# A single maximum in the second step of every unit of a two-branch attention kernel

## The chip, the cores and the metric

One Trainium2 chip, one core of it. The metric is the device time of the kernel in microseconds (us). The kernel before takes 1472.81 us, the median of 3 runs from 1471.78 to 1473.0 us.

## The reference

Two attention branches read the same input `x` of 2048 rows by 512 columns and are mixed by a gate per row. Branch A is a dilated window attention (each row sees 8 keys, every second row back). Branch B, which fills most of the time, is full attention of 32 query heads of 16 columns on one shared key head and one shared value head:

```python
def _A_ref(x, wqkv, wo):                       # 32 heads of 16, W, dil = 8, 2
    idx = pos[:, None] - off[None, :]          # off = arange(8) * 2
    logits = jnp.einsum("bhsd,bhswd->bhsw", q, kg) * scale
    o = jnp.einsum("bhsw,bhswd->bhsd", _softmax(logits), vg)
    return o @ wo
def _B_ref(x, wq, wk, wv, wo):                 # 32 query heads, one key and one value head
    scores = jnp.einsum("bhqd,bkd->bhqk", q, k) * (Dh ** -0.5)
    o = jnp.einsum("bhqk,bkd->bhqd", _softmax(scores), v)
    return o @ wo
g = _sigmoid((x * gate_w).sum(-1, keepdims=True))
return g * a + (1 - g) * b
```

The weights of branch B's queries and keys are 8 times the others, so its scores are large, and the kernel subtracts each row's own maximum before the exponential.

## The kernel before, in words

**Stages.** A front part (until about 284 us in the trace) splits the inputs into a high and a low part, projects queries, keys and values, and begins the maxima. A long loop then does branch B step by step, with branch A's arithmetic on GpSimd (POOL) beside it. Three times in the loop a block of output projections (`out_phase`) is put between two steps, and a short tail projects the last rows.

**Units and steps.** Branch B is cut into 32 units: a unit is 512 query rows of 4 heads. A unit has 16 steps, one for each block of 128 keys, so the loop runs over `s` from 0 to 512 with `u, kt = divmod(s, 16)`. The engines' work of one step is recorded in this order:

- two times the scores of a pair of heads, two matmuls into the bank pair `pe` (L465), which ScalarE turns into `pexp` with one exponential of 128x1024 (L471);
- between the first and the second of these the maxima of a later unit: always, where slots are left, a *pair* of maxima, two matmuls into `pm` (L322) and one reduction of 128x1024 on VectorE (`fill_pair`, L344), and sometimes a *single* maximum, one matmul into `ps` (L322) and one reduction of 128x512 (`fill_one`, L356);
- at the end the weighted sums of the step before, eight matmuls into `po` (L480), which accumulate over the 16 steps of a unit. In the trace one `po` row of eight matmuls therefore closes each step, and the time from one such row to the next is the length of a step.

**The turn of a unit.** In step `s % 16 == 0` the sixteenth weighted sum of the old unit is recorded and right behind it `finish_a`: VectorE transposes `po` to `tt` (L494) and takes a reciprocal (L500). The first weighted sum of the new unit, at the end of step `s % 16 == 1`, may overwrite `po` only when that transpose has read it. I call step `s % 16 == 1` the turn step, and count turns by the unit that begins: turn 14 is step 225.

**When a unit's maxima are complete** (64 slots, counted in `left`), `filled` puts a small reduction (`ms`, L332) and a transpose (`mt`, L334) on VectorE; ScalarE and GpSimd make the shift rows of it, and eight small DMAs write them into the unit's query tile.

**What sets the order.** Nothing is scheduled after recording: each engine works its list in the order in which the Python code records it. That order comes from a planner. `clk` holds a guess of each engine's time, `free[bank]` the time at which a bank may be written again, `slots` and `half` the maxima that are still to be done. In the loop `order` is (first scores, "m2", "m1", second scores): "m2" is the pair, "m1" the single. The single is given out when `singles(s)` says yes and the bank `ps` is free by the planner's clock; each one given lowers `owing` by 1. `singles` adds to `owing`, at every step, the maxima left beyond what the pairs of the remaining steps (1.94 each) and the coming output blocks (15.5 a row block) will take, divided by the steps left. It says no in step 0 of a unit, where `owing` is below 1, and where the planner has VectorE over 1.5 us behind TensorE while `owing` is below 2. In the turn step the pair's reduction stands behind the transpose on VectorE, so the planner has VectorE far behind there, and that last rule decides.

A place where DMAs are issued within the loop is `run_tasks` (the shift rows, L453, and query loads, L290 and L291, on SyncE's queue) and `run_pool` (branch A); both run by the planner's clock.

Of the kernel before, what the change touches and what calls it, by code (L numbers as in the profile page):

```python
# [48 lines left out]
def gated_mix_kernel(ctx, tc, xt, wa, wk, wq, wo_a, wo_b, out):  # L49
# [274 lines left out]
    def to_go():  # L324
        return 2 * len(slots) + len(half)
# [519 lines left out]
    def singles(s):  # L845

        steps = 16 * (NU - 1) - 8 - s
        if steps <= 0 or to_go() <= 0:
            return to_go() > 0
        owing[0] += (to_go() - 1.94 * steps - 15.5 * (NJ - 4 - outs)) / steps  # L850
        owing[0] = min(owing[0], 3.0)
        if s % 16 == 0 or owing[0] < 1.0 or clk["dve"] - clk["pe"] > 1.5 and owing[0] < 2.0:
            return False
        return True
# [373 lines left out]
    for s in range(NS + 1):  # L1228
# [29 lines left out]
        for which in order:  # L1258
            if which == "m2":
                if slots or half:  # L1260
                    fill_ready("m2", M2S)
                else:
                    next(tail, None)
            elif which == "m1":
                if singles(s) and fill_ready("m1", M1S):
                    owing[0] -= 1.0
            elif s < NS:
                exp_pair(s, which)
# [84 lines left out]
```

## Time and profile before

| | |
|---|---|
| median of 3 runs | 1472.81 us |
| the profiled execution | 1471.12 us, span 1469.1 us |
| busy: TensorE, VectorE, ScalarE, GpSimd | 1454.6, 1141.9, 1303.6, 951.1 us |
| clock granted to TensorE | 1.0 throughout |
| exponentials of branch B | 1024, 1.02 us each |
| transposes of `po` at a turn | 31, 0.72 us each |

In the timeline a row is a run of like instructions: start and length in us, engine, line, operation, output and inputs, and how many; a bracket at its end gives the idle time before it and what ended that. PE is TensorE, PEld its weight loads, DVE VectorE, ACT ScalarE. Matmuls are pipelined, so a TensorE that is shown as busy all the time may still be waiting inside a step; the length of a step is read from the starts.

### The profile page before, as it was taken

How to read it: one execution, taken by the hardware profiler on the slowest of the kernel's cores; microseconds unless marked ns; L12 is line 12 of the kernel's file. 1: busy time of each engine (PE TensorE's matmuls, PEld its weight loads, DVE VectorE, ACT ScalarE, POOL GpSimd, SP SyncE). 2: the span in 40 equal slices, each digit the busy share in tenths (PEclk: the TensorE clock that was granted, in tenths of full speed). 3: DMA queues.
4: the chain of work that ended last, by engine and by line, in shares of the span. 5: the costliest groups of instructions: out<-in, count | busy, mean ns of one | idle time of the engine just before them, and what ended most of it. 6: DMA issues, size and time to landing. Idle time of an engine off the chain costs nothing.

```text
span 1469.1 us, 29512 instructions
## 1 busy us (share of the span) xinstructions
PE 1454.6 (99%) x10965; PEld 739.7 (50%) x10965; DVE 1141.9 (78%) x1837; ACT 1303.6 (89%) x1706; POOL 951.1 (65%) x1693
## 2 busy tenths in 40 slices
PE   9999999999999999999999999999999999999998
PEld 6899999733333333333333373333333743383334
DVE  6778888788888888788888877888888778778821
ACT  5888988799999999999999989999999889889994
POOL 5731898888988988889888898898851311150000
PEclk9999999999999999999999999999999999999999
DMA  6653342320211210102202111121100000000000
GB/s 225 170 169 113 101 149 68 117 73 25 71 41 49 78 49 31 68 22 69 78 12 71 42 63 46 45 71 41 42 12 12 27 16 2 1 31 1 1 2 29
DMA packets 43912, 85.67 MB, mean 58 GB/s; under 512 B 9520, under 2 KB 25960, under 8 KB 39672
## 3 DMA queue, kind: packets, MB, share of 16 engines
q1 hardware_dynamic: 36632, 44.79, 9.9%
q0 software_dynamic: 6560, 37.95, 7.7%
q8 instruction: 86, 1.41, 0.4%
q10 hardware_dynamic: 576, 1.05, 0.2%
q14 instruction: 58, 0.48, 0.1%
HBM read 57.97 MB, written 25.25 MB: 57 GB/s over the span
## 4 chain that ended last, share of the span: by engine, by line
PE 94%; ACT 2%; POOL 1%; DVE 1%; DMA 1%; issue 1%; SPq 0%; POOLq 0%; ACTq 0%
PE po L480 34%; PE pe L465 25%; PE pf L1082 10%; PE pm L322 8%; PE ps L322 5%; PE pe L780 5%; PE pd L393 3%; PE po L322 1%; ACT pexp L471 1%; PE pf L193 1%; PE pe L1283 1%; DMA ad<-stage 0%; DVE mx L344 0%; DMA xraw<-xt 0%; PE pm L836 0%
## 5 line engine op out<-in xcount | busy, mean ns | idle before, releaser
L471 ACT ACTIVATE pexp<-pe 128x1024 f32<-128x1024 f32 x1024 | 987.8, 1023 | 67.6 <-PE pe L465 63.3
L344 DVE TENSOR_REDUCE mx<-pm 128x2 f32<-128x1024 f32 x475 | 580.1, 1221 | 174.6 <-PE pm L322 172.3
L480 PE MATMUL po<-pexp,vst 128*32 128x512 f32 x4096 | 545.5, 605 | 0.1
L465 PE MATMUL pe<-qst,kst 64*128 64x512 f32 x1984 | 523.3, 459 | 4.6 <-ACT pexp L471 2.5
L465 PEld LDWEIGHTS pe<-qst,kst 64*128 64x128 f32 x1984 | 208.8, 183 | 451.6 <-ACT pexp L471 427.2
L405 ACT ACTIVATE dd<-pd 128x512 f32<-128x512 f32 x367 | 209.0, 604 | 44.7 <-PE pd L393 30.9
L356 DVE TENSOR_REDUCE mx<-ps 128x1 f32<-128x512 f32 x333 | 226.5, 680 | 4.5 <-PE ps L322 1.8
L322 PE MATMUL ps<-kst,qst 62*128 62x512 f32 x503 | 206.5, 410 | 0.1
L322 PE MATMUL pm<-kst,qst 62*128 62x512 f32 x916 | 185.9, 397 | 0.4
L542 POOL TENSOR_TENSOR pr<-aext 128x256 f32<-128x256 f32 x256 | 182.0, 737 | 4.9 <-DMA aext<-ad 4.6
L602 POOL TENSOR_TENSOR oa<-oa,av 128x256 f32<-128x256 f32 x224 | 164.1, 732 | 15.8
L480 PEld LDWEIGHTS po<-pexp,vst 128*32 128x32 f32 x4096 | 80.6, 108 | 170.3 <-issue 161.8
L417 DVE CUSTOM_DVE_ANT_0 dd<-ps,dd 128x512 f32<-128x512 f32 x185 | 127.7, 690 | 34.2 <-PE ps L322 14.2
L417 DVE CUSTOM_DVE_ANT_0 dd<-po,dd 128x512 f32<-128x512 f32 x182 | 125.6, 690 | 29.8 <-PE po L322 12.9
L599 POOL TENSOR_TENSOR av<-aext,lg 128x256 f32<-128x256 f32 x224 | 139.3, 622 | 12.8
L393 PE MATMUL pd<-kd,qst 62*128 62x512 f32 x367 | 143.5, 401 | 2.5 <-ACT dd L405 2.5
L1082 PE MATMUL pf<-wal,xh 64*128 64x384 f32 (+1 forms) x496 | 127.9, 338 | 0.0
L1082 PE MATMUL pf<-wah,xh 64*128 64x384 f32 (+1 forms) x496 | 124.0, 337 | 0.0
L1082 PE MATMUL pf<-wah,xl 64*128 64x384 f32 (+1 forms) x496 | 122.7, 338 | 0.0
L322 PEld LDWEIGHTS ps<-kst,qst 62*128 62x128 f32 x503 | 92.9, 185 | 43.5 <-DVE mx L356 38.6
L506 POOL TENSOR_TENSOR rl<-rl,gate_t 128x16 f32<-128x16 f32 x31 | 6.9, 222 | 157.9 <-DVE rl L500 157.9
L322 PEld LDWEIGHTS pm<-kst,qst 62*128 62x128 f32 x916 | 88.3, 186 | 3.5 <-DVE mx L344 3.0
(199 smaller groups left out, 1725.4 us busy)
## 6 DMA issues: line engine op xcount, KB each, us to landing
aext<-ad POOLq DMA_DIRECT2D x32, 1056.0 KB, 5.4
ad<-stage SPq DMA_DIRECT2D x32, 384.0 KB
qst<-qd SPq DMA_DIRECT2D x62, 128.0 KB
xraw<-xt SPq DMA_DIRECT2D x16, 256.0 KB
qd<-qhi SPq DMA_DIRECT2D x16, 256.0 KB
qd<-qlo SPq DMA_DIRECT2D x16, 256.0 KB
qst<-qd SPq DMA_DIRECT2D x62, 64.0 KB
qst<-ml SPq DMA_DIRECT2D x220, 2.0 KB
```

Of the source, the lines that this page charges most:

```text
L322: nc.tensor.matmul(dst, qst[place(v)][b:b + 62, pr, t * P:(t + 1) * P], kst[b:b + 62, kc * 512:(kc + 1) * 512], start=True, stop=True)
L344: got = nc.vector.tensor_reduce(m[:, :, pr, t, kc], dst, AX.X, ALU.max)
L356: got = nc.vector.tensor_reduce(m[:, odd, pr, t, kc:kc + 1], dst, AX.X, ALU.max)
L393: nc.tensor.matmul(dst, qst[place(v)][b:b + 62, pr, t * P:(t + 1) * P], kd[0][b:b + 62, kc // 2, :], start=True, stop=True)
L405: got = nc.scalar.activation(held[b][k], dst, AF.Relu)
L417: got = nc.vector.tensor_tensor_reduce(held[b][k], dst, held[b][k], 1.0, -FMAX, ALU.add, ALU.max, m[:, b, pr, t, kc:kc + 1])
L465: nc.tensor.matmul(bank[:, odd, :], kst[b:b + 64, kt * P:(kt + 1) * P], qst[place(u)][b:b + 64, pr, :], start=True, stop=True)
L471: got = nc.scalar.activation(e, bank, AF.Exp, scale=SCALE)
L480: nc.tensor.matmul(po[32 * i:32 * i + 32, :], vst[:, kt, :], pexp[s, i // 2][:, i % 2, :], start=(kt == 0), stop=(kt == NJ - 1))
L542: nc.gpsimd.tensor_mul(pr[:, k], q, e[:, o:o + NH, AC:2 * AC])
L602: nc.gpsimd.tensor_add(ao, ao, av)
L1082: inst = nc.tensor.matmul(home(x)[0][:, :n], l[h], r[h], start=(i == 0 and b == 0), stop=(i == 3 * C - 1 and b == 1))
```

## The change

In `singles`, a step with `s % 16 == 1` says yes before the other rules are asked:

```diff
         owing[0] += (to_go() - 1.94 * steps - 15.5 * (NJ - 4 - outs)) / steps
         owing[0] = min(owing[0], 3.0)
+        if s % 16 == 1:
+            return True
         if s % 16 == 0 or owing[0] < 1.0 or clk["dve"] - clk["pe"] > 1.5 and owing[0] < 2.0:
             return False
         return True
```

Counted in the recorded programs, the change does this. There are 30 turn steps in which maxima are left; three of them follow an output block and had a single before and after. Of the other 27, 9 had a single before, and all 27 have one now. Outside the turn steps the loop has fewer singles: 300 before and 273 after in the steps 17 to 486, without the nine steps around the output blocks. In all, singles in `ps` go from 325 to 316, full pairs from 475 to 480, half-filled pair banks from 10 to 7, and the three output blocks take 66, 57 and 60 maxima before and 59, 66 and 60 after. The output blocks stay at steps 272, 400 and 448, and the last maximum at step 488.

TensorE around turn 14, before; the first row is the last weighted sums of the old unit, and `ps` is the single:

```order
L480 MATMUL po<-pexp,vst 32x512 x4
L465 MATMUL pe_4182<-qst_80,kst 128x512 x2
L322 MATMUL pm<-kst,qst_77 128x512 x2
L465 MATMUL pe_4183<-qst_80,kst 128x512 x2
L480 MATMUL po<-pexp,vst 32x512 x4
L465 MATMUL pe_4182<-qst_80,kst 128x512 x2
L322 MATMUL pm<-kst,qst_77 128x512 x2
L322 MATMUL ps<-kst,qst_77 128x512
L465 MATMUL pe_4183<-qst_80,kst 128x512 x2
L480 MATMUL po<-pexp,vst 32x512 x4
```

The same place after:

```order
L480 MATMUL po<-pexp,vst 32x512 x4
L465 MATMUL pe_4182<-qst_80,kst 128x512 x2
L322 MATMUL pm<-kst,qst_77 128x512 x2
L322 MATMUL ps<-kst,qst_77 128x512
L465 MATMUL pe_4183<-qst_80,kst 128x512 x2
L480 MATMUL po<-pexp,vst 32x512 x4
L465 MATMUL pe_4182<-qst_80,kst 128x512 x2
L322 MATMUL pm<-kst,qst_77 128x512 x2
L465 MATMUL pe_4183<-qst_80,kst 128x512 x2
L480 MATMUL po<-pexp,vst 32x512 x4
```

The single stood in the step behind the turn step and stands now in the turn step itself, ahead of the second scores.

VectorE around turn 15, before; `tt<-po` is the transpose for which the new unit's first weighted sum waits, and `ms` and `mt` are what a completed unit of maxima puts on the engine:

```order
L356 TENSOR_REDUCE mx<-ps 128x1
L344 TENSOR_REDUCE mx<-pm 128x2
L494 STREAM_TRANSPOSE tt<-po 128x512
L500 RECIPROCAL rl<-tt 128x16
L344 TENSOR_REDUCE mx<-pm 128x2
L332 TENSOR_REDUCE ms<-mx 128x32
L334 STREAM_TRANSPOSE mt<-ms 128x32
L344 TENSOR_REDUCE mx<-pm 128x2
```

The same place after:

```order
L356 TENSOR_REDUCE mx<-ps 128x1
L344 TENSOR_REDUCE mx<-pm 128x2
L332 TENSOR_REDUCE ms<-mx 128x32
L334 STREAM_TRANSPOSE mt<-ms 128x32
L494 STREAM_TRANSPOSE tt<-po 128x512
L500 RECIPROCAL rl<-tt 128x16
L344 TENSOR_REDUCE mx<-pm 128x2
L356 TENSOR_REDUCE mx<-ps 128x1
```

The unit's maxima are now complete one step earlier, so `ms` and `mt` stand ahead of the transpose. They stand so at turns 3 and 6 before, and at turns 3, 6, 9, 12 and 15 after; at 3, 6 and 12 the reduction ahead of them is a half pair, at 9 and 15 a full one.

Branch A's small reductions on VectorE, the shift rows and the query loads move by some rows with the planner's clock; their number stays.

## The prediction

> **What bounds the kernel now.** I began with the page, then read the loop by windows, the waits, and last the timeline of TensorE and VectorE around several turns. Of the page, two lines, and under them one row of the windows by stage (busy time and count of TensorE, its weight loads, VectorE, ScalarE, GpSimd, then the granted clock):
>
> ```profile
> span 1469.1 us, 29512 instructions
> ...
> L471 ACT ACTIVATE pexp<-pe 128x1024 f32<-128x1024 f32 x1024 | 987.8, 1023 | 67.6 <-PE pe L465 63.3
> ```
>
> ```profile
> 460.00:560.00 100.00, 100.00 (x709) 35.93 (x709) 82.71 (x101) 94.72 (x105) 87.48 (x169) 1.00 0.17 55
> ```
>
> TensorE is shown busy all the time at full clock, ScalarE for 94.7 of 100 us and VectorE for 82.7. So neither of the two others is full, and ScalarE's 67.6 us of idle time ahead of its exponentials is mostly time in which it waits for TensorE's scores. TensorE's busy share doesn't say how much it waits inside a step; the starts do. This is the timeline of TensorE around turn 14, where the turn step has no single:
>
> ```profile
> 748.60 1.06 PE L480 MATMUL po<-pexp,vst 128*32 128x512 f32 x8
> ...
> 749.93 0.39 PE L322 MATMUL pm<-kst,qst 62*128 62x512 f32 x2
> 750.16 0.40 PE L465 MATMUL pe<-qst,kst 64*128 64x512 f32 x2
> 750.49 1.07 PE L480 MATMUL po<-pexp,vst 128*32 128x512 f32 x8
> ...
> 751.83 0.39 PE L322 MATMUL pm<-kst,qst 62*128 62x512 f32 x2
> 752.15 0.49 PE L465 MATMUL pe<-qst,kst 64*128 64x512 f32 x2
> 752.57 1.06 PE L480 MATMUL po<-pexp,vst 128*32 128x512 f32 x8
> ...
> 754.14 0.39 PE L322 MATMUL ps<-kst,qst 62*128 62x512 f32 x1
> ...
> 754.70 1.06 PE L480 MATMUL po<-pexp,vst 128*32 128x512 f32 x8
> ...
> 756.27 0.45 PE L322 MATMUL ps<-kst,qst 62*128 62x512 f32 x1
> ...
> 756.88 1.06 PE L480 MATMUL po<-pexp,vst 128*32 128x512 f32 x8
> ```
>
> From one `po` row to the next is one step. The step of 750.49 has no single and takes 750.49 - 748.60 = 1.89 us. The turn step has the same matmuls and takes 752.57 - 750.49 = 2.08. The two steps behind it each have a single and take 2.13 and 2.18. So the turn step loses 0.19 us without doing anything for it: its second scores begin 0.32 behind the pair instead of 0.23 (they wait for ScalarE to empty their bank), and its weighted sums begin 0.42 behind those scores instead of 0.33 (they wait for the transpose of `po`). Two rows of the waits name both:
>
> ```profile
> PEld pe L465 <- ACT pexp L471: 441.2, 562, 1.7
> ...
> PEld po L480 <- DVE tt L494: 6.8, 25, 0.4
> ```
>
> Now turn 5, which already carries a single in the turn step:
>
> ```profile
> 448.07 1.06 PE L480 MATMUL po<-pexp,vst 128*32 128x512 f32 x8
> ...
> 449.97 1.06 PE L480 MATMUL po<-pexp,vst 128*32 128x512 f32 x8
> ...
> 451.54 0.39 PE L322 MATMUL ps<-kst,qst 62*128 62x512 f32 x1
> ...
> 452.09 1.06 PE L480 MATMUL po<-pexp,vst 128*32 128x512 f32 x8
> ...
> 453.99 1.06 PE L480 MATMUL po<-pexp,vst 128*32 128x512 f32 x8
> ```
>
> Its three steps take 1.90, 2.12 and 1.90 us. The single is in the turn step and costs 0.04 there, and the step behind it, now without one, takes 1.90. That is the change in small, within the trace of before.
>
> **The change part by part.** All sums are against the profiled execution's own 1471.12 us (span 1469.1 and 2.0 around it). The median is 1.7 above that; I subtract the same sum from it.
>
> *Singles that enter a turn step: 18.* These are the first and the last of the 18 turn steps without one, each with a step with a single behind it:
>
> ```profile
> 315.96 1.07 PE L480 MATMUL po<-pexp,vst 128*32 128x512 f32 x8
> ...
> 318.05 1.06 PE L480 MATMUL po<-pexp,vst 128*32 128x512 f32 x8
> ...
> 320.19 1.06 PE L480 MATMUL po<-pexp,vst 128*32 128x512 f32 x8
> ```
>
> ```profile
> 1381.40 1.07 PE L480 MATMUL po<-pexp,vst 128*32 128x512 f32 x8
> ...
> 1383.51 1.07 PE L480 MATMUL po<-pexp,vst 128*32 128x512 f32 x8
> ...
> 1385.63 1.06 PE L480 MATMUL po<-pexp,vst 128*32 128x512 f32 x8
> ...
> 1387.53 1.07 PE L480 MATMUL po<-pexp,vst 128*32 128x512 f32 x8
> ```
>
> They take 2.09 and 2.11, over the 18 a mean of 2.10. The nine turn steps with a single take 2.12 to 2.14, a mean of 2.13. So 18 x 0.03 = +0.5 us.
>
> *Singles that leave other steps: 27.* Outside the turn, the steps with a single take 2.14 where the step before has none (113 of them; above 2.14, 2.13, 2.12) and 2.17 where it has one (185; above 2.18), together 2.16. The 134 steps without take 1.91 (above 1.89, 1.90, 1.90). A single is worth 0.25 there. Of the 27, 25 stood beside a pair: -25 x 0.25 = -6.3. The other two stood alone, where no pair was ready, and become steps with a pair alone: about -0.1 together. 18 of the 27 are the ones that moved to the turn. The other nine are no longer needed as singles, since five more steps have a full pair, three fewer have a half one, and the output blocks take two more maxima.
>
> *The output blocks: two maxima more.* The 916 matmuls of pairs bound that:
>
> ```profile
> L322 PE MATMUL pm<-kst,qst 62*128 62x512 f32 x916 | 185.9, 397 | 0.4
> ```
>
> 185.9 / 916 = 0.20 us each on TensorE; between 0, if they fill gaps of the block, and 0.4. I take +0.2.
>
> *VectorE in the turn step.* Its queue is what the single's reduction joins. VectorE at turn 5, with the single:
>
> ```profile
> 449.85 1.23 DVE L344 TENSOR_REDUCE mx<-pm 128x2 f32<-128x1024 f32 x1 [0.31 <-PE pm L322]
> 451.11 0.72 DVE L494 STREAM_TRANSPOSE tt<-po 128x512 f32<-128x512 f32 x1
> 451.86 0.25 DVE L500 RECIPROCAL rl<-tt 128x16 f32<-128x16 f32 x1
> 452.03 1.16 DVE L344 TENSOR_REDUCE mx<-pm 128x2 f32<-128x1024 f32 x1
> 453.11 0.67 DVE L356 TENSOR_REDUCE mx<-ps 128x1 f32<-128x512 f32 x1
> 453.86 1.23 DVE L344 TENSOR_REDUCE mx<-pm 128x2 f32<-128x1024 f32 x1
> 455.75 1.23 DVE L344 TENSOR_REDUCE mx<-pm 128x2 f32<-128x1024 f32 x1 [0.66 <-PE pm L322]
> ```
>
> The single's reduction stands behind the transpose, so the weighted sums do not wait for it. Behind it on the engine stand the next step's pair and whatever needs `pm` and `ps` again. The work from the transpose to the end of the next step's pair is 0.72 + 0.25 + 1.16 + 0.67 + 1.23 = 4.03 us, against 2.12 + 1.90 = 4.02 of TensorE for these two steps: VectorE comes out even, and two steps later it is idle for 0.66 us again. I take the cost at nothing; the cover is that the step behind has no single, which holds in all 27 turns after. Without that cover it is a wait of up to one reduction, 0.67. The Trainium skill's page "TensorEngine Tiling (Array Packing)", section "PSUM Bottleneck", says that tiling speeds up TensorE but not the emptying of PSUM, which can then become the bottleneck; by that rule the turn would be paid by VectorE, and the sum would lose what the first rival below takes from it. The nine turns with a single speak against it: the steps behind them take a mean of 1.91, like any other step without one.
>
> *The transpose comes later at two turns.* At turns 9 and 15 `ms` and `mt` are now ahead of `tt`, behind a full pair. Turn 6 shows them behind a half pair:
>
> ```profile
> 482.92 0.69 DVE L356 TENSOR_REDUCE mx<-pm 128x1 f32<-128x512 f32 x1
> 483.65 0.29 DVE L332 TENSOR_REDUCE ms<-mx 128x32 f32<-128x128 f32 x1
> 483.97 0.21 DVE L334 STREAM_TRANSPOSE mt<-ms 128x32 f32<-128x32 f32 x1
> 484.19 0.72 DVE L494 STREAM_TRANSPOSE tt<-po 128x512 f32<-128x512 f32 x1
> ```
>
> From the end of the half pair, 483.61, to the transpose they take 0.58. A full pair is 0.54 longer than a half one, and after it the transpose starts at once (451.08 and 451.11 above), so it comes some 0.55 later at these two turns. With the single as cover, 0.1 of that may be hidden: 2 x 0.45 = +0.9, between 0 and 1.1. At turn 12 the pair is a half one, and nothing is lost.
>
> *Other queues.* Query loads and shift rows swap places by a few rows on SyncE's queue, and branch A's pieces move on GpSimd's. They are meant for units that start several steps later, so I take nothing for them, between -0.5 and +1.
>
> *The steps with a single that are left.* They stand behind another single less often, 151 of 273 instead of 185 of 298, so that their mean is (122 x 2.14 + 151 x 2.17) / 273 = 2.157 instead of 2.159: 273 x 0.002 = -0.5.
>
> The sum: 0.5 - 6.3 - 0.1 + 0.2 + 0.9 - 0.5 = -5.3. That is 1465.8 us for a run like the profiled one, and 1472.8 - 5.3 = **1467.5** for the median.
>
> **The rivals.**
>
> *VectorE pays (the same time).* Where branch A's small reductions fall between the turn and the next steps, VectorE does not come out even, and the next pair or single waits for its bank. If each of the 18 new turn singles cost a full 0.25 in that way, 4.5 of the 5.3 us come back: 1472.8 - 0.8 = 1472.0. For it: the 4.03 against 4.02 above. Against it: the steps behind the nine turns, and the 0.66 us of idle time right after. The rule of the skill's page named above points here.
>
> *ScalarE is the limit (slower).* The single stands ahead of the second scores, so the second exponential of the turn step can start 0.23 later. If ScalarE has no slack to catch up, the single costs its full 0.25 there, 18 x 0.25 = +4.5. Steps that lose a single then run into ScalarE's pace: a plain step behind a plain step takes 2.08 at turn 14, not 1.91, so that 27 removed singles bring only 27 x (2.16 - 2.08) = -2.2. With +0.2 and +0.9 that is +3.4, so 1476.2. It decides from where the exponentials follow each other without idle time over a whole unit. For it: ScalarE's 94.7 of 100 us. Against it: the 5.3 us that are left, which are spread over all units, and turn 5, where three steps in a row run at 1.90, 2.12 and 1.90.
>
> That the change does not do what it says can be left out: the order has the single in all 27 turn steps.
>
> **How the numbers follow.** My forecast gets 0.78, VectorE 0.14, ScalarE 0.08. The forecast's own range: without the late transposes and with the other queues at their good end it is -5.3 - 0.9 - 0.5 = -6.7, so 1466.1, and 1.7 lower, 1464.4, if the runs fall as the profiled one did; with the two maxima, the transposes and the queues at their bad ends it is -5.3 + 0.2 + 0.2 + 1 = -3.9, and if a quarter of the 5.3 is lost to what I don't see, -2.6, so 1470.2. I take 1464.4 to 1471.2 as the range, which reaches a little towards VectorE's case. A measurement of this kernel can tell about 0.2% from no change, 2.9 us, so faster begins below 1469.9: 0.78, of which I give 0.02 to the same for the forecast's own upper end, so 0.76; the same 0.16 with VectorE's case; slower 0.08.
>
> **What would show it right or wrong.** In the profile after, the 18 turn steps should take 2.13 and the steps behind them 1.90; turns 9 and 15 some 2.5; 27 fewer steps of 2.16; ScalarE's idle time ahead of its exponentials should fall by some 5 us. I am wrong if the turn steps with a single take 2.3, if the steps behind them take 2.1 with a wait for L344 or L356 in front, or if plain steps elsewhere rise to 2.08.

## The result, and the profile after

| | before | after |
|---|---|---|
| median | 1472.99 us (1470.65 to 1474.68) | 1467.71 us (1465.41 to 1468.85) |
| ratio, 95% interval | | 0.9965 (0.9956 to 0.9974) |
| the profiled execution | 1471.12 us | 1466.79 us, span 1464.7 us |

The kernel is 5.3 us faster, by the medians of eight runs each. The page after, its span and the exponentials' group:

```profile
span 1464.7 us, 29500 instructions
...
L471 ACT ACTIVATE pexp<-pe 128x1024 f32<-128x1024 f32 x1024 | 986.8, 1023 | 64.2 <-PE pe L465 58.4
```

ScalarE's idle time ahead of its exponentials, behind TensorE's scores, went from 63.3 to 58.4 us. This is TensorE around turn 14 after the change, the `po` rows and the single:

```profile
746.36 1.07 PE L480 MATMUL po<-pexp,vst 128*32 128x512 f32 x8
...
748.25 1.06 PE L480 MATMUL po<-pexp,vst 128*32 128x512 f32 x8
...
749.82 0.40 PE L322 MATMUL ps<-kst,qst 62*128 62x512 f32 x1
...
750.38 1.07 PE L480 MATMUL po<-pexp,vst 128*32 128x512 f32 x8
...
752.27 1.06 PE L480 MATMUL po<-pexp,vst 128*32 128x512 f32 x8
...
754.39 1.06 PE L480 MATMUL po<-pexp,vst 128*32 128x512 f32 x8
```

The four steps take 1.89, 2.13 (the turn step, with its single), 1.89 and 2.12 us. Before, the same four took 1.89, 2.08, 2.13 and 2.18. VectorE at the same turn:

```profile
748.13 1.23 DVE L344 TENSOR_REDUCE mx<-pm 128x2 f32<-128x1024 f32 x1 [0.29 <-PE pm L322]
749.38 0.72 DVE L494 STREAM_TRANSPOSE tt<-po 128x512 f32<-128x512 f32 x1
...
751.38 0.67 DVE L356 TENSOR_REDUCE mx<-ps 128x1 f32<-128x512 f32 x1
752.15 1.23 DVE L344 TENSOR_REDUCE mx<-pm 128x2 f32<-128x1024 f32 x1
```

The single's reduction stands behind the transpose, as the order says, and the next pair's reduction starts at 752.15, 0.1 behind its end.

I took every step's length from the starts of the `po` rows over the whole loop: steps 17 to 486 without the nine around the output blocks, 461 steps, as in the prediction. Number x mean, in us:

| steps | before | after |
|---|---|---|
| turn step, plain | 18 x 2.097 | none |
| turn step with a single | 9 x 2.127 | 27 x 2.147 |
| other step with a single, behind a plain step | 113 x 2.143 | 122 x 2.141 |
| other step with a single, behind one with a single | 185 x 2.172 | 151 x 2.182 |
| other step with a single but no pair | 2 x 1.984 | none |
| plain step, behind one with a single | 125 x 1.898 | 151 x 1.903 |
| plain step, behind a plain step | 9 x 2.077 | 10 x 2.055 |
| sum | 960.7 | 956.6 |

The 151 steps hold one of 3.71 us. The same step takes 2.12 in a second profile of the change, so it costs some 1.6; it is the granted clock that falls there, as the last section shows. Without it the loop gains 5.7 us. From profiled execution to profiled execution the 4.4 us of span are: -5.7 in these steps, +1.6 by the long step, +0.5 in the output blocks, -0.2 up to the first `po` row, and the -0.5 that is left in the first 15 steps, beside the blocks, in the last steps and in the tail.

### The profile page after: what moved, and what is told of

It reads as the page before. It is cut to its first block, busy times and chain, and to the rows that moved or that the text cites. A ratio compares the mean times of both kernels' runs of the same rounds, so it can differ in the third digit from the quotient of the medians.

```text
span 1464.7 us, 29500 instructions
## 1 busy us (share of the span) xinstructions
PE 1451.1 (99%) x10965; PEld 742.0 (51%) x10965; DVE 1140.7 (78%) x1832; ACT 1303.8 (89%) x1708; POOL 950.9 (65%) x1693
## 4 chain that ended last, share of the span: by engine, by line
PE 95%; ACT 1%; POOL 1%; DVE 1%; DMA 1%; issue 0%; SPq 0%; POOLq 0%; ACTq 0%
PE po L480 34%; PE pe L465 25%; PE pf L1084 10%; PE pm L322 8%; PE ps L322 6%; PE pe L780 5%; PE pd L393 3%; PE po L322 1%; PE pf L193 1%; PE pe L1285 1%; ACT pexp L471 1%; DVE mx L344 0%; DMA ad<-stage 0%; DMA xraw<-xt 0%; PE pm L836 0%
## 5 line engine op out<-in xcount | busy, mean ns | idle before, releaser
L471 ACT ACTIVATE pexp<-pe 128x1024 f32<-128x1024 f32 x1024 | 986.8, 1023 | 64.2 <-PE pe L465 58.4
L344 DVE TENSOR_REDUCE mx<-pm 128x2 f32<-128x1024 f32 x480 | 586.5, 1222 | 173.8 <-PE pm L322 169.7
L465 PE MATMUL pe<-qst,kst 64*128 64x512 f32 x1984 | 515.7, 459 | 4.4 <-ACT pexp L471 2.6
L465 PEld LDWEIGHTS pe<-qst,kst 64*128 64x128 f32 x1984 | 204.1, 184 | 454.6 <-ACT pexp L471 424.8
L356 DVE TENSOR_REDUCE mx<-ps 128x1 f32<-128x512 f32 x323 | 219.7, 680 | 2.8 <-PE ps L322 2.8
L322 PE MATMUL ps<-kst,qst 62*128 62x512 f32 x494 | 202.0, 409 | 0.1
```

What stands on the lines that cost most here:

```text
L322: nc.tensor.matmul(dst, qst[place(v)][b:b + 62, pr, t * P:(t + 1) * P], kst[b:b + 62, kc * 512:(kc + 1) * 512], start=True, stop=True)
L344: got = nc.vector.tensor_reduce(m[:, :, pr, t, kc], dst, AX.X, ALU.max)
L356: got = nc.vector.tensor_reduce(m[:, odd, pr, t, kc:kc + 1], dst, AX.X, ALU.max)
L465: nc.tensor.matmul(bank[:, odd, :], kst[b:b + 64, kt * P:(kt + 1) * P], qst[place(u)][b:b + 64, pr, :], start=True, stop=True)
L471: got = nc.scalar.activation(e, bank, AF.Exp, scale=SCALE)
```

## The experiments

Each was run beside the kernel before, on one chip per group; a ratio is to the kernel before in the same group. "Singles" are the single maxima, and the edits are in the planner's rule that gives them out.

**The place or the number? Two kernels.** The change also makes the singles more regular and fewer. The first kernel forbids them in the turn step:

```diff
         if s % 16 == 1:
-            return True
+            return False
```

> No unit's turn step has a single at all (27 of 27 without, before 18 of 27); the planner gives 328 singles elsewhere (before 325) and four maxima fewer in the output blocks. My theory (a single costs 0.03 us in a turn step and 0.25 elsewhere): 9 turn steps lose 0.03 each, some 12 more ordinary steps carry a single at 0.25, four maxima fewer in the blocks at 0.12: +2.2 us, so 1475.2 against 1473.0 before. Rival, the gain came from the planner's other changes and not from the place: 1472.5 to 1473.5.

Measured: 1475.67 us (1474.12 to 1478.24), ratio 1.0026 (1.0017 to 1.0036), 3.5 slower than before. The turn steps are plain in all 27 turns. At turn 10 step 0 of the unit takes unusually long; TensorE there, `po` rows alone:

```profile
615.00 1.07 PE L480 MATMUL po<-pexp,vst 128*32 128x512 f32 x8
...
617.28 1.06 PE L480 MATMUL po<-pexp,vst 128*32 128x512 f32 x8
...
619.18 1.07 PE L480 MATMUL po<-pexp,vst 128*32 128x512 f32 x8
```

617.28 - 615.00 = 2.28 for step 0, and 1.90 for the plain turn step behind it. Four of the 27 turns are like this (10, 16, 20 and 23, with 2.06 to 2.28 and then 1.90 to 1.92). So a turn step without a single need not take 2.08; that was the first sign against a part of my reading.

The second kernel forces a single in the middle of the unit instead:

```diff
-        if s % 16 == 1:
+        if s % 16 == 8:
```

> The same forced single, but in the ninth step of each unit, far from the turn; the turn steps follow the old rules (7 of 27 with a single). My theory: no place is gained, 1473.0 to 1474.0. Rival, a regular single in any fixed step evens out the planner's bookkeeping and that is the gain: 1467 to 1468.5.

Measured: 1473.62 us (1472.72 to 1475.42), ratio 1.0012 (1.0003 to 1.0021). The turn steps stay at 20 x 2.078 and 7 x 2.110 us and the steps' sum is 962.4. As regular as the change, and slower than before: regularity alone brings nothing. The number of singles is not held apart here (311 in the 461 steps, 309 before, 300 in the change); the kernel with the late transposes below does that.

**VectorE left out of it.** The change as it is, but the single of the turn step gets no reduction (31 reductions fewer; TensorE's list stays the same):

```diff
+        if bare:
+            after("dve", after("pe", 0, T_R) + T_LAT, T_RED1)
+            free[key] = clk["dve"] + 0.08
+            filled(v, 1)
+            return
...
+                bare[:] = [1] * (s % 16 == 1)
```

> As the changed kernel, but the reduction of the single given in a turn step is left out (31 reductions of 128x512 on VectorE, so those maxima are missing from the result); TensorE's list is the same. My theory (VectorE takes the turn's single at almost no cost): 0 to 0.8 us faster than the changed kernel, 1466.9 to 1467.7. Rival, VectorE pays for the turn's singles: a further 2 to 4.5 us faster, 1463.2 to 1465.7.

Measured: 1466.68 us (1465.74 to 1468.18), ratio 0.9964 (0.9952 to 0.9977); the change itself has 0.9965. TensorE at turn 14 (the weighted sums are L487 in this file):

```profile
749.80 1.06 PE L487 MATMUL po<-pexp,vst 128*32 128x512 f32 x8
...
751.37 0.40 PE L322 MATMUL ps<-kst,qst 62*128 62x512 f32 x1
...
751.93 1.07 PE L487 MATMUL po<-pexp,vst 128*32 128x512 f32 x8
...
753.83 1.07 PE L487 MATMUL po<-pexp,vst 128*32 128x512 f32 x8
```

2.13 and 1.90 us, within 0.01 of what the full change takes there, and 27 turn steps at a mean of 2.148, with 1.932 for the steps behind them (2.147 and 1.933 in the change). The reduction is hidden, and the rival in which VectorE pays for the turn's single is out. The Trainium skill's rule that emptying PSUM can become the bottleneck ("TensorEngine Tiling (Array Packing)", section "PSUM Bottleneck") does not bind in the change.

**A single in step 0 as well.** If singles are cheap at a turn, two may be cheaper, unless the reduction ahead of the transpose delays it:

```diff
-        if s % 16 == 1:
+        if s % 16 < 2:
```

> A single is given in the first step of a unit as well as in the second. Its reduction of 0.68 us then stands ahead of the transpose of the finished sums. My theory: the singles that leave other steps save about 7.5 us against before, but the turn's weighted sums wait some 0.5 to 0.65 longer in 27 turns (+13 to +17): 1479 to 1483. Rival, only TensorE's count matters and VectorE's queue at the turn does not: 1465 to 1466.

Measured: 1468.81 us (1468.0 to 1470.9), ratio 0.9979 (0.997 to 0.9988). I had expected some ten more: a miss. VectorE and TensorE around turn 14:

```profile
750.90 1.23 DVE L344 TENSOR_REDUCE mx<-pm 128x2 f32<-128x1024 f32 x1 [0.30 <-PE pm L322]
752.04 0.68 DVE L356 TENSOR_REDUCE mx<-ps 128x1 f32<-128x512 f32 x1
752.64 0.71 DVE L494 STREAM_TRANSPOSE tt<-po 128x512 f32<-128x512 f32 x1
```

```profile
751.32 1.06 PE L480 MATMUL po<-pexp,vst 128*32 128x512 f32 x8
...
753.45 1.07 PE L480 MATMUL po<-pexp,vst 128*32 128x512 f32 x8
```

The old unit's last weighted sums run from 751.32 to 752.38, and no transpose can start before they end. The single's reduction runs from 752.04, so only its end lies on the path: the transpose starts 1.32 behind the start of the sums' row, where after the change alone it is 1.13, and not a whole reduction later. The turn step takes 2.13 us, and 2.177 in the mean of 26. By the ratios the kernel is still 2 us slower than the change. Step 0 with its single takes 2.16 us in the mean where the plain one takes 1.94, nearly the 0.25 of any other step, and the step behind the turn takes 2.01 instead of 1.93.

**What does the plain turn step wait for?** I had read its 2.08 us as two waits, for ScalarE and for the transpose. Reading A: the transpose is part of it. Reading B: it is a plain step behind a plain step, and ScalarE paces two of these in a row. To tell them apart the turn step stays plain and step 0, ahead of it, always has the single; in a second kernel the reductions of those singles are left out, so that they cannot delay the transpose:

```diff
-        if s % 16 == 1:
-            return True
+        if s % 16 < 2:
+            return s % 16 == 0
```

> A single in the first step of each unit and never in the turn step (27 turn steps plain, each behind a step with a single; 331 singles in all). It asks why a plain turn step takes 2.08 us: reading A, because the transpose of the sums holds it up; reading B, because it is a plain step behind a plain step, and ScalarE's two exponentials cannot keep up with two such steps in a row. The single's reduction stands ahead of the transpose here, which by the run with singles in both steps puts the transpose some 0.2 us later. Reading A: turn steps of 2.1 to 2.3, the kernel at 1473.5 to 1477. Reading B: turn steps of 2.0 to 2.1, 1468.5 to 1472.

Measured: 1476.5 us (1475.18 to 1478.18), ratio 1.0028 (1.0018 to 1.0039); the plain turn steps take 27 x 2.123. That looks like reading A. But VectorE shows another delay at turn 14:

```profile
753.31 0.68 DVE L356 TENSOR_REDUCE mx<-ps 128x1 f32<-128x512 f32 x1
753.91 0.71 DVE L494 STREAM_TRANSPOSE tt<-po 128x512 f32<-128x512 f32 x1
```

The `po` row of step 0 starts at 752.57 there, so the transpose starts 1.34 behind it, 0.2 later than before (751.62 - 750.49 = 1.13), because of the reduction ahead. The kernel alone decides nothing; with those reductions left out it does:

> The same order on TensorE, with the reduction of the singles of the first steps left out (so those maxima are missing from the result) and the transpose no longer behind it. Reading A, the transpose holds up a plain turn step: still 2.07 to 2.10. Reading B, two plain steps in a row do: the turn step falls to 1.90 to 1.93, and the kernel is 3 to 5 us faster than with the reductions.

Measured: 1472.81 us (1470.27 to 1473.51), ratio 0.9997 (0.9988 to 1.0006), 3.7 us faster than with the reductions, and the plain turn steps take 27 x 1.919. Turn 9 in this kernel (transpose L501, weighted sums L487), and the transpose at turn 14 in the kernel before:

```profile
585.61 0.72 DVE L501 STREAM_TRANSPOSE tt<-po 128x512 f32<-128x512 f32 x1 [0.25 <-PE po L487]
```

```profile
584.48 1.06 PE L487 MATMUL po<-pexp,vst 128*32 128x512 f32 x8
...
586.38 1.06 PE L487 MATMUL po<-pexp,vst 128*32 128x512 f32 x8
```

```profile
751.62 0.72 DVE L494 STREAM_TRANSPOSE tt<-po 128x512 f32<-128x512 f32 x1
```

In both the transpose starts 1.13 us behind the old unit's last `po` row. In the one the turn step takes 586.38 - 584.48 = 1.90, in the other 2.08. What differs is the step ahead: with a single here, plain there. So the length of the turn step goes by reading B. Before's own trace could have told it: the transpose ends at 752.34 and the weighted sums start at 752.57, 0.23 later. And its nine plain steps behind a plain one away from the turn, where nothing waits for a transpose, have the two gaps that the prediction split between two waits: 0.32 from the pair to the second scores and 0.43 from there to the weighted sums, in the mean, against 0.34 and 0.43 in the plain turn steps. ScalarE in the kernel before over step 0 and the turn step of turn 14:

```profile
750.16 3.81 ACT L471 ACTIVATE pexp<-pe 128x1024 f32<-128x1024 f32 x4 [0.20 <-PE pe L465]
```

Four exponentials follow each other without a pause, and the weights of the turn step's second scores wait 0.32 us for one of them; at turn 9 in the kernel without those reductions they wait for none. The row of waits named the transpose all the same, and in this kernel, where the turn steps take 1.92, it is larger than the 6.8 us of before:

```profile
PEld po L487 <- DVE tt L501: 9.1, 28, 0.4
```

The transpose is not free, though. Most of what the turn step saves here against the kernel before, the step behind it pays. This is VectorE behind the transpose of turn 9, and then the pair of the step behind on TensorE:

```profile
586.53 1.16 DVE L344 TENSOR_REDUCE mx<-pm 128x2 f32<-128x1024 f32 x1
```

```profile
587.75 0.57 PE L322 MATMUL pm<-kst,qst 62*128 62x512 f32 x2
...
588.64 0.64 PE L487 MATMUL po<-pexp,vst 128*32 128x512 f32 x4
```

The pair starts when the reduction behind the transpose has emptied its bank, at 587.69, and the step takes 588.64 - 586.38 = 2.26. A plain turn step and a step with pair and single behind it take 1.92 and 2.26 in the mean of 19 turns here, and 2.10 and 2.13 in 16 turns before: 4.19 against 4.23 together. The change escapes this because its step behind the turn has no single.

**The late transposes taken away.** `ms` and `mt` are recorded behind the turn's transpose whenever a unit's maxima are completed in step 0:

```diff
+            if turning:
+                late.append(v)
+            else:
+                close(v)
...
+        turning.clear()
+        while late:
+            close(late.pop(0))
```

> As the changed kernel, but where a unit's maxima become complete in the first step of another unit, the small reduction and transpose for it are recorded behind the turn's transpose of the sums, not ahead of it. The planner then gives 324 singles instead of 316 (27 in turn steps as before, 282 instead of 273 in the other steps between 17 and 486). My theory prices place and number apart: turns 9 and 15 fall from 2.32 to 2.13 (-0.4), nine singles more in other steps cost 0.25 each (+2.3), two maxima fewer in the blocks (-0.2): 1.5 to 2 us slower than the changed kernel. Rival, the place in the turn is the whole gain and the number of singles does not matter: 0.4 faster than the changed kernel.

Measured: 1469.12 us (1468.41 to 1469.7), ratio 0.9979 (0.997 to 0.9988), 2.4 slower than the change in the same group. Turn 15 falls from 2.32 to 2.12 us, as it should. But the planner's clock moves, and 282 steps outside the turn have a single instead of 273 (at turns 9 and 12 the single stands beside a half pair, and the step takes 1.90 and 1.91). Nine more singles at 0.25 are 2.2, and the late transposes are small against that.

This kernel also parts the place from the number. It has 309 singles in the 461 steps, as many as the kernel before, and its output blocks take 101.8 us, as before; what differs is where the singles stand. It is 2.9 us faster than before by the medians, and its steps sum to 958.6 instead of 960.7. So the place brings 2 to 3 us, and the nine singles fewer bring the change about as much again.

**The change again,** in the group of the next two:

> The changed kernel once more, beside the next three on one chip: 1466 to 1468, ratio to before about 0.9965.

Measured: 1466.68 us (1465.73 to 1469.0), ratio 0.9966 (0.9954 to 0.9978). Its profile has no long step in the loop: the steps sum to 954.8, 5.9 below before, and the blocks again take 0.5 more. It reaches the first `po` row at 285.04 instead of 284.21, but there the granted clock is at half for 3.4 us from 216.4 us on.

**Singles into the idle time behind the output blocks.** TensorE stands idle twice behind each block, so a maximum should be free there. First one, in the step behind a block, then one more in the unused bank `po`:

```diff
-        if s % 16 == 1:
+        if s % 16 == 1 or fresh:
...
+                if fresh and (slots or half) and fillable():
+                    fill_one(po, "po")
+                    owing[0] -= 1.0
```

> As the changed kernel, with a single also in the step right behind each of the three output blocks (steps 272, 400, 448), where TensorE stands idle for 0.64 and 0.41 us while ScalarE empties the last output and does the first exponential, and where the transpose is long done. My theory: three singles move from a step where they cost 0.25 to one where they cost nothing: 0.5 to 0.8 us faster than the changed kernel. If the shorter idle time also keeps the clock of TensorE up in the 3 us behind the block, where the profile of the changed kernel shows it at 0.50 once, up to 1.7 us more.

> As the run with a single behind each output block, with a second one there in the idle bank of the weighted sums. If these steps still hold idle time, again 0.5 to 0.8 us faster; if the transposed bank's reduction delays the first weighted sum of the unit, nothing or a little slower. Clock dips behind the blocks rarer if the idle time is their cause.

Measured: 1466.58 us (1465.61 to 1467.46), ratio 0.9961 (0.9949 to 0.9974), with one; 1466.34 us (1464.98 to 1467.15), ratio 0.9958 (0.9946 to 0.9971), with two. TensorE behind the second block in the change (idle time in the brackets), and then with one:

```profile
1179.62 0.51 PE L465 MATMUL pe<-qst,kst 64*128 64x512 f32 x2 [0.64 <-ACT two L678]
1180.54 0.50 PE L465 MATMUL pe<-qst,kst 64*128 64x512 f32 x2 [0.41 <-ACT pexp L471]
```

```profile
1180.28 0.50 PE L465 MATMUL pe<-qst,kst 64*128 64x512 f32 x2 [0.32 <-ACT two L678]
```

The first idle time is filled, from 0.64 to 0.32 us and to none with two; the second stays at 0.41. But the 0.1 to 0.3 us by which the medians fall cannot be told from no gain, where I had expected 0.5 to 0.8 from each of the two kernels: a miss. The loop has three and five singles fewer than with the change alone (297 and 295 in the 461 steps), and the steps sum to 954.8 and 954.3 against 954.8, so these singles were not worth 0.25 each; why is open. The kernel with two has the lowest median of all, and is not shown to beat the change.

## Why the prediction was right, and where it was not

Forecast 1467.5 us, measured 1467.7: the sum of -5.3 came out to the tenth in the medians. The mechanism held, but the tenth is luck: the interval of the ratio leaves 3.8 to 6.5 us, and the terms miss by 0.1 to 0.5, in both directions. By its terms:

| term | predicted | measured |
|---|---|---|
| 18 singles enter turn steps | +0.5 | +0.7: turn steps 56.9 to 58.0 us in all, without turns 9 and 15's delay |
| late transposes, turns 9 and 15 | +0.9 | +0.4 in the turn steps, and +0.3 in the steps behind them, which the next row holds |
| singles leave other steps (-6.3, -0.1, -0.5) | -6.9 | -6.8: steps with a single 647.9 to 589.1 (the long step's 1.6 taken out), plain ones 255.9 to 307.9 |
| two maxima more in the blocks | +0.2 (0 to 0.4) | +0.5: 101.8 to 102.3 us |
| VectorE in the turn step | 0 | none seen, by leaving the reductions out |
| other queues | 0 (-0.5 to +1) | -0.2 up to the first `po` row; the second profile's +0.8 holds the drop of the clock at 216.4 us |

*The nine old turns as a model for the 18 new ones* held: 2.12 to 2.14 us in the turn steps, but for turns 3, 9 and 15, and 1.89 to 1.92 in 21 of the 27 steps behind them. The other six take 1.99 to 2.13, so that the mean is 1.93 and not 1.90. Turn 3 took 2.30 before and after.

*Place and number were priced together.* By the prediction's prices the place of 18 singles is worth 18 x (0.25 - 0.03) = 4.0 us and the nine singles fewer 2.2. The kernel with as many singles as before shows 2 to 3 for the place, so the place gave less, and the number more, than these prices say; one kernel shows this, and it has its own order of singles.

*Why the turn step was long is the step that failed.* The prediction put part of its lost 0.19 us to the transpose of `po`. The wait's row should then have shrunk with the plain turn steps. The waits after:

```profile
PEld pe L465 <- ACT pexp L471: 438.2, 550, 1.7
...
PEld po L480 <- DVE tt L494: 7.1, 22, 0.5
```

It is 7.1 us against 6.8 before. What makes the step long is ScalarE's pace over two plain steps in a row, as the kernel without step 0's reductions showed: 1.92 us with the transpose no earlier. The numbers came out all the same, because a single in the turn step breaks the pair of plain steps, whichever wait made that pair long.

*The late transposes were mis-sized.* Turn 9 after, on TensorE and on VectorE:

```profile
581.77 1.07 PE L480 MATMUL po<-pexp,vst 128*32 128x512 f32 x8
...
584.09 1.06 PE L480 MATMUL po<-pexp,vst 128*32 128x512 f32 x8
...
586.12 1.06 PE L480 MATMUL po<-pexp,vst 128*32 128x512 f32 x8
```

```profile
581.64 1.23 DVE L344 TENSOR_REDUCE mx<-pm 128x2 f32<-128x1024 f32 x1
582.90 0.29 DVE L332 TENSOR_REDUCE ms<-mx 128x32 f32<-128x128 f32 x1
583.23 0.21 DVE L334 STREAM_TRANSPOSE mt<-ms 128x32 f32<-128x32 f32 x1
583.36 0.67 DVE L494 STREAM_TRANSPOSE tt<-po 128x512 f32<-128x512 f32 x1
```

The transpose starts 1.59 behind the start of the old unit's last sums instead of 1.13, later by 0.46 where I had said 0.55. And it ends at 584.03 and the sums start at 584.09: the delay first uses up most of the 0.28 us that lie between the two at turn 14 (750.10 and 750.38), and about 0.19 is left, in a turn step of 2.32 where I said some 2.5. I had counted 0.1 of cover. The step behind takes 2.03 instead of 1.90.

*The blocks were mis-sized.* Two maxima more brought 0.47, above my bound of 0.4. The blocks' lengths go with the maxima in each: 57, 60 and 66 take 33.41, 33.90 and 34.50 before; 59, 66 and 60 take 33.89, 34.51 and 33.88 after. From 57 to 59 maxima a block takes 0.48 longer, from 60 to 66 only 0.6: I gave every maximum the same price, and by these six lengths it is not the same.

*The rivals.* VectorE does not pay for the turn's single, as shown. ScalarE as the limit gave slower steps where two plain ones meet; they do take 2.06 to 2.08 there, but outside the turn there are 10 such steps after and 9 before, while the 18 plain turn steps are gone. Its idle time fell by 4.9 us, about the 5 that I had named. So ScalarE's pace, which the prediction held against the change, is what made the turn step a cheap place.

## What to carry to other kernels

Price a filler by the step it enters and by what the step ahead carries: here the same matmul costs 0.25 us in a step behind one that has it or not, and some 0.04 where it breaks up two light steps that another engine paces anyway. A row of waits names what came last, not what would come next (the transpose's row was 6.8 us before and 9.1 where the turn step had become short); before a term is built on it, look whether the time between the releaser's end and the start of the waiter is nothing, as it is at turn 9 (0.06) and was not at turn 14 (0.23). And a delayed instruction costs only what is left of the delay beyond the slack that it had: a reduction of 0.68 ahead of the transpose moved it by 0.2 us.

## What the runs showed of the hardware

The step of 3.71 us in the loop after is a drop of the granted clock. The windows of 1 us behind the second output block (after the window: its length, busy time and count of TensorE, its weight loads, VectorE, ScalarE and GpSimd, then the granted clock):

```profile
1181.00:1182.00 1.00, 1.00 (x11) 0.37 (x11) 0.68 (x1) 1.00 (x2) 0.01 (x1) 0.99 0.20 76
1182.00:1183.00 1.00, 1.00 (x8) 0.06 (x6) 1.00 (x2) 1.00 (x2) 0.00 (x0) 0.50 0.50 186
...
1184.00:1185.00 1.00, 1.00 (x6) 0.81 (x7) 0.02 (x1) 0.44 (x1) 0.00 (x0) 0.50 0.05 16
1185.00:1186.00 1.00, 1.00 (x7) 0.23 (x9) 1.00 (x1) 0.81 (x2) 0.00 (x0) 0.80 0.00 0
```

```profile
1181.89 1.90 PE L480 MATMUL po<-pexp,vst 128*32 128x512 f32 x8
...
1185.60 1.06 PE L480 MATMUL po<-pexp,vst 128*32 128x512 f32 x8
```

The clock is at half for some 3.4 us, and eight weighted sums take 1.90 instead of 1.06. All that TensorE had been idle in the 10 us before are the 0.64 and 0.41 us shown above. The Trainium skill's page "TensorE: Matmul & The Clock Gate" asks in "HAM oscillation — how this bites in real kernels" for no idle gap above about 3.4 us; the half rate agrees, but no gap of that length lies ahead of this drop. The Trainium skill also says there, in its section on PSUM-queue depth-cycling, that frequent short idle times can do it too, and gives no length for them. The gaps alone do not bring it here: at the same place the kernel before has 0.66 and 0.42 us, and the second profile of the change 0.65 and 0.41, with the clock at 1.00 behind them. What brings it stays open.

The kernel before has such drops too. Of its 27 runs in one group, three had a mean clock of 1.000 and took 1470.97 us in the mean, 22 had 0.999 and took 1472.31, and two had 0.998 and took 1473.93: one drop is worth about 1.4 us. Of the twelve profiles kept, five have one behind an output block, six have one in the front part at 216 to 218 us (three have both), and four have none. Where it falls into the front part, the first `po` row starts at 285.0 to 285.5 us, elsewhere at 284.0 to 284.6.

The drops are not equally frequent in all kernels: 0.998 or less stands in 8 of 61 runs of the kernel before, beside the experiments, and in 9 of 14 of the change. So some of the gain seems to be lost to them. The change's one run at 1.000 took 1465.41 us, 5.7 less than the mean of the six runs of before at 1.000 (1471.06), where the medians differ by 5.3. Why the change should have more of them is not shown. Nor is it shown that filling the idle time behind the blocks makes them rarer: the two kernels that fill it still had 0.998 and 0.999.
